# Rotated order of matmul groups over two array halves, value blocks ahead of projections, rings cleared later, in a fused attention and gated-MLP kernel

## Chip, cores and metric

One core of one Trainium2 chip runs the kernel. The metric is device time in microseconds (us) of one launch; a profiled execution gives a trace with every engine's instructions.

## The reference

For 2048 tokens of width 512 (x) the kernel mixes two branches with a gate per token, `g = sigmoid(sum(x * gate_w))`:

```python
qkv = x @ wqkv                       # 32 heads of 16
p = softmax(q k^T / 4) where 0 <= i - j < 256
a = (p @ v) @ wo
b = (sigmoid(x @ w_gate) * (x @ w_up)) @ w_down   # inner width 1376
out = g * a + (1 - g) * b
```

## The kernel before

Float32 precision comes from splitting: each operand is a rounded high part and a low remainder (`split`: ScalarE casts the high part, VectorE subtracts), and a product is three matmuls (`mm3`). A contraction of 512 is four slices d of 128 rows, so a 512-column result takes 12 matmuls.

Instructions stand in the order in which the code issues them on TensorE (PE), ScalarE (ACT), VectorE (DVE) and SyncE (SP), whose queue holds all DMAs; GpSimd (POOL) masks and fills. Tags of PSUM pools name banks: `s` 2, `st` 2, `misc` 3, `pv` 1.

*Opening.* 20 filler matmuls on zeros (`idle_mm`) run until data comes. SP loads query/key weights `wqk`, chunk 0 of x (512 tokens, four slices), the value weights `wv`, then chunks 1 to 3 of x, all but `wqk` into the space of the later value tile V. GpSimd clears three rings (`ring`, stacked query and key rows), then writes V's constant columns (`fill_v`). PE projects step 0 and step 4 (`proj_mm`, tiles pj), with fillers between, computes value blocks 0 to 3 (`v_block`, tiles vps) and goes on with projection 1. A projection step is 512 tokens of one group of four heads' queries and keys; pairs of steps are copied into a ring by `stack_build` through SP (from tiles sh and sl, high and low).

*Main loop.* Round u (0 to 139) has four sub-rounds hh. Each issues one score matmul group for the row maximum (`s_part`, tile s, VectorE reduces it) for u below 128, and from u = 9 (LAG) one transposed score (`st_part`, tile st, ScalarE's exponential into pt). GpSimd masks pt (`mask_p`); every second round `pv_part` multiplies by V into the bank pv.

*Filler stream.* Between these, `turns()` feeds groups of 12 matmuls: gate and up products (gu), further projections (pj) and the remaining width (tail, tp). Each contraction slice is cut in two halves of 64 rows; half 0 uses the upper half of the array's rows and half 1 the lower, and both add into one bank of tag misc. At step t half 0 does its step t, half 1 the step t - SHIFT; GAP = 3 steps go out per `next(slots)`. There are n_rest = 111 groups:

```python
for half, v in enumerate((t, t - SHIFT)):
    if 0 <= v < n_rest * k3:
        groups[v // k3][0](v % k3, half)
```

A group's result is taken off its bank (`post`) once half 1 is through: by ScalarE for gu and pj, put at the front of the list `acts`, of which one entry is issued per sub-round. `gu_next` then splits the next block's weights into the single weight tile w0. At the end the last three tail groups run undivided (`hold_group`), and the second matrix products (pd, pa) follow for 44 steps.

## Time and profile before

| | us |
|---|---|
| median of 3 runs (742.84 to 743.03) | 742.88 |
| profiled execution, own time | 743.2 |
| its span, first to last instruction | 741.5 |
| PE busy | 735.4 |
| VectorE busy | 505.3 |
| ScalarE busy | 432.2 |
| GpSimd busy | 173.9 |

Matmuls are pipelined and their ends are modelled: the time of one is read from the distance of starts, not from its length. Of a wait for several semaphores the profile names the last.

### The profile page before, as it was taken

The page shows a single profiled execution, that of the slowest core. Times are in us where ns is not written, and L with a number is a line of the kernel's source. Part 1 is how long each engine was busy: PE and PEld are TensorE (multiplying, and loading weights), DVE is VectorE, ACT ScalarE, POOL GpSimd, SP SyncE. Part 2 cuts the span into 40 slices and gives each one's busy share as a digit, 9 for nine tenths or more (in the row PEclk, how much of TensorE's full clock was granted, in tenths as well). Part 3 has the DMA queues.
Part 4 walks back from the last instruction along what each step waited for, and adds up shares of the span by engine and source line. Part 5 has one row for each costly group of instructions (what it writes and reads, how often), then busy time and mean ns, then how long its engine had stood idle before and what let it go on. Part 6 is the DMA issues. An engine that isn't in the chain of part 4 may idle for free.

```text
span 741.5 us, 17721 instructions
## 1 busy us (share of the span) xinstructions
PE 735.4 (99%) x6310; PEld 586.3 (79%) x6310; DVE 505.3 (68%) x1518; ACT 432.2 (58%) x921; POOL 173.9 (23%) x256
## 2 busy tenths in 40 slices
PE   9999999999999999999999999999999999999997
PEld 7889777787777877778777787778887878887886
DVE  5358767766776776776677677677745774848473
ACT  6422676666676666666666666666665662535341
POOL 7000333233233223323323322332341000000000
PEclk9999999999999999999999999999999999999999
DMA  8341434436444353443534425554277867879561
GB/s 299 102 120 30 108 96 119 128 85 166 122 107 127 106 147 111 115 130 96 155 111 120 122 72 155 154 140 138 72 267 221 238 174 193 203 180 228 146 133 58
DMA packets 94321, 103.66 MB, mean 140 GB/s; under 512 B 44926, under 2 KB 57214, under 8 KB 94232
## 3 DMA queue, kind: packets, MB, share of 16 engines
q1 hardware_dynamic: 94232, 102.53, 50.0%
q8 instruction: 49, 0.80, 0.4%
q14 instruction: 40, 0.33, 0.1%
HBM read 45.32 MB, written 31.99 MB: 104 GB/s over the span
## 4 chain that ended last, share of the span: by engine, by line
PE 96%; DMA 2%; DVE 1%; issue 0%; ACT 0%; SPq 0%; DVEq 0%
PE gu L247 28%; PE pv L394 12%; PE pj L247 11%; PE s L315 8%; PE tp L519 5%; PE st L361 5%; PE pd L80 5%; PE pd L78 5%; PE pd L79 5%; PE vh L556 3%; PE pa L78 2%; PE pa L79 2%; PE pa L80 2%; DMA V<-in_xT_dram 2%; PE vps L78 1%; PE vps L79 1%
## 5 line engine op out<-in xcount | busy, mean ns | idle before, releaser
L321 DVE CUSTOM_DVE_ANT_0 junk<-s,mask 128x384 f32<-128x384 f32 (+2 forms) x512 | 271.7, 531 | 125.5 <-PE s L315 68.5
L366 ACT ACTIVATE pt<-st 128x384 f32<-128x384 f32 (+2 forms) x512 | 240.2, 473 | 168.0 <-PE st L361 68.6
L247 PE MATMUL gu<-xh,w 64*128 64x512 f32 x1152 | 295.3, 393 | 0.0
L247 PE MATMUL gu<-xl,w 64*128 64x512 f32 x576 | 190.7, 392 | 0.0
L371 POOL TENSOR_SCALAR_AFFINE_SELECT pt<-pt 128x512 f32<-128x512 f32 x128 | 88.1, 688 | 372.4 <-ACT pt L366 372.4
L247 PEld LDWEIGHTS gu<-xh,w 64*128 64x128 f32 x1152 | 160.9, 185 | 14.1
L361 PE MATMUL st<-ring 64*128 64x384 f32 (+2 forms) x536 | 168.5, 332 | 0.2 <-ACT ring L121 0.2
L315 PE MATMUL s<-ring 64*128 64x384 f32 (+2 forms) x536 | 167.0, 329 | 0.4 <-DVE mx L321 0.4
L315 PEld LDWEIGHTS s<-ring 64*128 64x128 f32 x536 | 95.6, 184 | 37.7 <-DVE nm L331 12.5
L361 PEld LDWEIGHTS st<-ring 64*128 64x128 f32 x536 | 96.6, 184 | 9.9 <-issue 2.7
L247 PEld LDWEIGHTS gu<-xl,w 64*128 64x128 f32 x576 | 90.7, 185 | 3.7
L394 PE MATMUL pv<-pt,V 128*32 128x384 f32 (+2 forms) x1408 | 91.0, 389 | 0.0
L247 PE MATMUL pj<-xh,wqh 64*128 64x512 f32 (+1 forms) x228 | 89.1, 397 | 0.0
L247 PE MATMUL pj<-xl,wqh 64*128 64x512 f32 (+1 forms) x228 | 88.3, 393 | 0.2 <-DVE xl L75 0.2
L376 POOL TENSOR_SCALAR_AFFINE_SELECT pt<-pt 128x512 f32<-128x512 f32 x112 | 76.2, 680 | 0.0
L247 PE MATMUL pj<-xh,wql 64*128 64x512 f32 (+1 forms) x228 | 69.9, 392 | 0.0
L394 PEld LDWEIGHTS pv<-pt,V 128*32 128x32 f32 x1408 | 37.2, 109 | 35.5 <-issue 29.2
L78 PE MATMUL pd<-ring,hb 128*128 128x512 f32 x160 | 63.0, 394 | 0.0
L80 PE MATMUL pd<-ring,hb 128*128 128x512 f32 x160 | 63.0, 393 | 0.0
L79 PE MATMUL pd<-ring,hb 128*128 128x512 f32 x160 | 62.3, 390 | 0.0
L74 ACT CAST hb<-V 128x512 fp32r<-128x512 f32 x40 | 24.9, 622 | 52.5 <-DVE V L703 50.0
L247 PEld LDWEIGHTS pj<-xl,wqh 64*128 64x128 f32 (+1 forms) x228 | 41.7, 185 | 3.4 <-DVE xl L75 1.4
(122 smaller groups left out, 1145.9 us busy)
## 6 DMA issues: line engine op xcount, KB each, us to landing
gu_scratch<-sp SPq DMA_DIRECT2D x72, 256.0 KB
V<-gu_scratch SPq DMA_DIRECT2D x36, 512.0 KB
ring<-sh SPq DMA_DIRECT2D x128, 128.0 KB
ring<-sl SPq DMA_DIRECT2D x64, 128.0 KB
guraw<-in_wgu_dram SPq DMA_DIRECT2D x18, 256.0 KB
V<-in_xT_dram SPq DMA_DIRECT2D x16, 256.0 KB
oT_scratch<-ob SPq DMA_DIRECT2D x128, 32.0 KB
xl<-oT_scratch SPq DMA_DIRECT2D x16, 256.0 KB
```

Of the source, the lines that this page charges most:

```text
L78: mm(ps, lh, rh, start=first, stop=False)
L79: mm(ps, lh, rl, start=False, stop=False)
L80: mm(ps, ll, rh, start=False, stop=last)
L247: mm(pt, (wl if w == 2 else wh)[r, d], (xl if w == 1 else xh)[r, d, c * CH:(c + 1) * CH], start=k == 0 and half != 1, stop=k == 3 * ND - 1 ...
L315: mm(pt[:, (k - k0) * P:(e - k0) * P], lhsT, blk(g, k, hh, 1, e - k), start=k == k0, stop=e == i + 1, skip_group_check=True,)
L321: nc.vector.tensor_tensor_reduce(junk[:, 0:n], pt[:, 0:n], mask[:, 3 * P - n:], scale=1.0, scalar=NEG, op0=ALU.add, op1=ALU.max, accum_out ...
L361: mm(pt[:, (q - j) * P:(e - j) * P], lhsT, blk(g, q, hh, 0, e - q), start=q == j, stop=e == last, skip_group_check=True,)
L366: nc.scalar.activation(pts[u][:, hh, 0:n], pt[:, 0:n], AF.Exp, scale=SCALE)
L371: nc.gpsimd.affine_select(p[:, :, 0:P], p[:, :, 0:P], pattern=[[0, HG], [1, P]], compare_op=ALU.is_ge, fill=0.0, base=0, channel_multiplie ...
L376: nc.gpsimd.affine_select(p[:, :, 2 * P:], p[:, :, 2 * P:], pattern=[[0, HG], [-1, P]], compare_op=ALU.is_gt, fill=0.0, base=0, channel_mu ...
L394: mm(pv[32 * hh:32 * hh + 32, (q % 4) * P:(q % 4 + e - q) * P], V[:, j, h * VW:h * VW + 32], p[:, hh, (q - j) * P:(e - j) * P], start=Fals ...
L519: mm(tp[b][:, 0:TW], (xl if w == 1 else xh)[r, d, b * P:(b + 1) * P], tw[d][int(w == 2)][r, 0:TW], start=k == 0 and half != 1, stop=k == 3 ...
```

## The change

Three things. *Opening:* wv and chunk 0 of x are loaded slice by slice in turn, the first x slice in two halves; value blocks 0 to 3 go first, in four banks at once, slice by slice; projections 0 and 4 follow without fillers, and 16 fillers instead of 20 stand ahead. *Rings:* GpSimd clears them behind the first `fill_v`, and the constant rows (`fill_rows(t, 1, 1)`) are written with each ring's first `stack_build`. *Rotation:* SHIFT is 6 instead of 18, groups are taken three at a time, and a table TURN gives each half its own order in a triple, (0, 2, 1) and (1, 0, 2), so that the halves never work on one group at the same time; a group is done when both halves are through, whichever was first. With that, projections are asked for in pairs (`proj_at`), and some of the last odd rounds take 3 steps less.

```diff
-SHIFT = 18
+SHIFT = 6
+TURN = ((0, 2, 1), (1, 0, 2))
...
-        idle_mm(20)
-
-        raw_q = load_wqk(0)
-        load_x(0, range(0, 2))
-        split_wqk(0, raw_q)
-        raw_q = load_wqk(1)
-        load_x(0, range(2, ND))
-        split_x(0, range(0, 2))
-        split_wqk(1, raw_q)
-        split_x(0, range(2, ND))
+        idle_mm(16)
+
         for d in range(ND):
             nc.sync.dma_start(wvraw[:, d], wv_v[:, d])
             split(wvh[:, d], wvl[:, d], wvraw[:, d])
+            for h in range(2) if d == 0 else (None,):
+                ts = slice(0, CH) if h is None else slice(h * CH // 2, (h + 1) * CH // 2)
+                nc.sync.dma_start(xraw[:, 0, d, ts], xT_v[:, d, ts])
+                split(xh[:, d, ts], xl[:, d, ts], xraw[:, 0, d, ts])
+        raw_q = [load_wqk(g) for g in range(2)]
         load_x(1)
-        split_x(1)
         load_x(2)
-        load_x(3)
+        for g in range(2):
+            split_wqk(g, raw_q[g])
+        split_x(1, range(0, 2))
+        load_x(3, range(0, 2))
...
-        for r in range(RING):
-            nc.gpsimd.memset(ring[r].bitcast(F32), 0.0)
-            nc.sync.dma_start(*fill_rows(r, 1, 1))
...
         fill_v(0, NB // 2)
+
+        for r in range(RING):
+            nc.gpsimd.memset(ring[r].bitcast(F32), 0.0)
...
             dmas = [fill_rows(t % RING, 0, 0)]
+            if t < RING:
+                dmas.append(fill_rows(t, 1, 1))
...
-        for s, k0, k1 in ((0, 0, 4), (NC, 0, 4), (0, 4, 6), (NC, 4, 6), (0, 6, 12), (NC, 6, 12)):
-            for k in range(k0, k1):
+        vq = [ps.tile([P, D], F32, tag=t, name=f"vps{b}", bufs=n)
+              for b, (t, n) in enumerate((("s", 2), ("s", 2), ("st", 2), ("misc", 3)))]
+        for d in range(ND):
+            for w in range(3) if d < ND - 1 else (None,):
+                for b in range(4):
+                    bs = slice(b * P, (b + 1) * P)
+                    for v in range(3) if w is None else (w,):
+                        mm(vq[b], (xl if v == 2 else xh)[:, d, bs], (wvl if v == 1 else wvh)[:, d],
+                           start=d == 0 and v == 0, stop=d == ND - 1 and v == 2)
...
+        v_out(0)
+        split_x(1, range(2, 3))
+        v_out(1)
+        split_x(1, range(3, ND))
+        load_x(3, range(2, ND))
+        v_out(2)
+        v_out(3)
+        for s in (0, NC):
+            for k in range(3 * ND):
                 proj_mm(s, k)
-                if s == 0 and k < 4:
-                    idle_mm(1 + k % 2)
...
-                if t % k3 == 0 and len(groups) < n_rest:
-                    groups.append((work or rest).pop(0))
+                if t % (3 * k3) == 0 and len(groups) < n_rest:
+                    groups.extend((work or rest).pop(0) for _ in range(3))
                 for half, v in enumerate((t, t - SHIFT)):
                     if 0 <= v < n_rest * k3:
-                        groups[v // k3][0](v % k3, half)
...
+                        n, k = divmod(v, k3)
+                        n += TURN[half][n % 3] - n % 3
+                        groups[n][0](k, half, n in halves_done)
+                        if k == k3 - 1:
+                            halves_done[n] = halves_done.get(n, 0) + 1
+                            if halves_done[n] == 2:
...
+        proj_at = {5: [5], LAG: [6, 7], U_LAST: [NSTEP - 2], U_LAST + 1: [NSTEP - 1]}
+        for s in range(8, NSTEP - 2):
+            proj_at.setdefault(4 * s - (20 if s % 2 else 17), []).append(s)
...
-                    if u >= NU:
+                    if u >= NU and not (hh == HG - 1 and u % 2 == 1 and u > NU + 1):
                         next(slots, None)
```

The opening on PE, behind the first fillers; pj are projections, vps value blocks, w the high part of wv. Before:

```order
L247 MATMUL pj_183<-xh,wqh_111 128x512
L185 MATMUL warm_ps<-warm 128x256
L247 MATMUL pj_183<-xl,wqh_111 128x512
L185 MATMUL warm_ps<-warm 128x256 x2
L247 MATMUL pj_183<-xh,wqh_111 128x512
L185 MATMUL warm_ps<-warm 128x256
L247 MATMUL pj_183<-xl,wqh_111 128x512
L185 MATMUL warm_ps<-warm 128x256 x2
L247 MATMUL pj_194<-xh,wqh_123 128x512
```

and now:

```order
L438 MATMUL vps_173<-w_72,xh 128x512
L438 MATMUL vps_174<-w_72,xh 128x512
L438 MATMUL vps_175<-w_72,xh 128x512
L438 MATMUL vps_176<-w_72,xh 128x512
L438 MATMUL vps_173<-wvl,xh 128x512
L438 MATMUL vps_174<-wvl,xh 128x512
L438 MATMUL vps_175<-wvl,xh 128x512
L438 MATMUL vps_176<-wvl,xh 128x512
L438 MATMUL vps_173<-w_72,xl 128x512
```

Value blocks stand where projections and fillers were, four blocks to a slice.

The end of the filler stream on PE, ahead of and around the last transposed scores (st127); tp are tail groups. Before, half 1 ends alone:

```order
L361 MATMUL st126_1_9553<-ring_63 128x256
L519 MATMUL tp11_9432<-tail_hb0_7805,xh_70 128x450
L519 MATMUL tp11_9432<-tail_hb0_7805,xl_71 128x450
L519 MATMUL tp11_9432<-tail_hb0_7805,xh_70 128x450
L519 MATMUL tp11_9432<-tail_hb1_7806,xh_70 128x450
L519 MATMUL tp11_9432<-tail_hb1_7806,xl_71 128x450
L519 MATMUL tp11_9432<-tail_hb1_7806,xh_70 128x450
L361 MATMUL st126_2_9566<-ring_63 128x256
```

and now at the same place both halves run:

```order
L362 MATMUL st126_1_9546<-ring_63 128x256
L537 MATMUL tp11_9414<-tail_hb0_7814,xh_70 128x450
L537 MATMUL tp12_9442<-tail_wqh0_7810,xh_70 128x450
L537 MATMUL tp11_9414<-tail_hb0_7814,xl_71 128x450
L537 MATMUL tp12_9442<-tail_wqh0_7810,xl_71 128x450
L537 MATMUL tp11_9414<-tail_hb0_7814,xh_70 128x450
L537 MATMUL tp12_9442<-tail_wql0_7811,xh_70 128x450
L537 MATMUL tp11_9414<-tail_hb1_7815,xh_70 128x450
```

The 18 lone steps have become 6, of which three stand ahead of st127's first pair and three between its pairs. The matmuls of a step, one per half, follow each other, tp11 and tp12 in turn.

GpSimd's fillers, before:

```order
L217 MEMSET fr 1x1024
L220 MEMSET ring 128x4x1024 x3
L224 MEMSET V 128x8x16
L225 MEMSET V 128x8x32
L224 MEMSET V 128x8x16
```

and now:

```order
L217 MEMSET fr 1x1024
L220 MEMSET V 128x8x16
L221 MEMSET V 128x8x32
L226 MEMSET ring 128x4x1024 x3
L220 MEMSET V 128x8x16
```

The three ring fillers have moved behind the first pair of V's.

More of the change, by code (lines that the diff above doesn't have):

```diff
@@ L242, in gated_mix_kernel, with group_mm @@
         stg = {}
-        def group_mm(pt, wh, wl, c, k, half):
+        def group_mm(pt, wh, wl, c, k, half, second):
             d, w = divmod(k, 2) if k < 2 * ND else (k - 2 * ND, 2)
@@ L247, in group_mm, with proj_mm @@
             mm(pt, (wl if w == 2 else wh)[r, d], (xl if w == 1 else xh)[r, d, c * CH:(c + 1) * CH],
-               start=k == 0 and half != 1, stop=k == 3 * ND - 1 and half != 0,
+               start=k == 0 and not second, stop=k == 3 * ND - 1 and (half is None or second),
                skip_group_check=half is not None)
-        def proj_mm(s, k, half=None):
+        def proj_mm(s, k, half=None, second=False):
             g, c = divmod(s, NC)
@@ L254, in proj_mm @@
                 pj[s] = ps.tile([P, CH], F32, tag="misc", name=f"pj{s}", bufs=3)
-            group_mm(pj[s], *wq[g], c, k, half)
+            group_mm(pj[s], *wq[g], c, k, half, second)
         def proj_raw(s):
@@ L428, in v_block, with v_out @@
                 v_part(b, d)
-        for s, k0, k1 in ((0, 0, 4), (NC, 0, 4), (0, 4, 6), (NC, 4, 6), (0, 6, 12), (NC, 6, 12)):
-            for k in range(k0, k1):
+        vq = [ps.tile([P, D], F32, tag=t, name=f"vps{b}", bufs=n)
[7 more added lines that the diff above has]
+                           start=d == 0 and v == 0, stop=d == ND - 1 and v == 2)
+        def v_out(b):
+            nc.scalar.copy(Vh[:, b, :, 0:DH], vq[b].rearrange("p (h w) -> p h w", w=DH))
+        v_out(0)
[7 more added lines that the diff above has]
+            for k in range(3 * ND):
                 proj_mm(s, k)
-                if s == 0 and k < 4:
-                    idle_mm(1 + k % 2)
         proj_hi(0)
@@ L437, in gated_mix_kernel @@
         proj_raw(NC)
-        v_block(0)
-        v_block(1)
-        v_block(2)
-        v_block(3)
         proj(1)
@@ L473, in gated_mix_kernel, with gu_mm @@
         gp = {}
-        def gu_mm(f, c, w, k, half=None):
+        def gu_mm(f, c, w, k, half=None, second=False):
             if (f, c, w) not in gp:
                 gp[f, c, w] = ps.tile([P, CH], F32, tag="misc", name=f"gu{f}_{c}_{w}", bufs=3)
-            group_mm(gp[f, c, w], gv[:, 0, w], gv[:, 1, w], c, k, half)
+            group_mm(gp[f, c, w], gv[:, 0, w], gv[:, 1, w], c, k, half, second)
         def gu_post(f, c, w):
@@ L485, in gu_post @@
                 load_gu(f + 1, w)
+        gu_left = {}
         def gu_next(f, c, w):
-            if f + 1 < NFM and c == NC - 1:
+            gu_left[f, w] = gu_left.get((f, w), NC) - 1
+            if f + 1 < NFM and gu_left[f, w] == 0:
                 split_gu(f + 1, w)
@@ L512, in tail_split, with tail_mm @@
             behind.append(lambda: nc.vector.tensor_tensor(lo, raw, hi.bitcast(F32), op=ALU.subtract))
-        def tail_mm(b, k, half=None):
+        def tail_mm(b, k, half=None, second=False):
             if b not in tp:
@@ L519, in tail_mm @@
             mm(tp[b][:, 0:TW], (xl if w == 1 else xh)[r, d, b * P:(b + 1) * P], tw[d][int(w == 2)][r, 0:TW],
-               start=k == 0 and half != 1, stop=k == 3 * ND - 1 and half != 0,
+               start=k == 0 and not second, stop=k == 3 * ND - 1 and (half is None or second),
                skip_group_check=half is not None)
@@ L585, in gated_mix_kernel @@
             (
-                lambda k, h=None, a=(f, c, w): gu_mm(*a, k, h),
+                lambda k, h=None, x=False, a=(f, c, w): gu_mm(*a, k, h, x),
                 lambda a=(f, c, w): gu_next(*a),
@@ L591, in gated_mix_kernel @@
         ] + [
-            (lambda k, h=None, b=b: tail_mm(b, k, h), None, lambda b=b: tail_post(b)) for b in range(NB)
+            (lambda k, h=None, x=False, b=b: tail_mm(b, k, h, x), None, lambda b=b: tail_post(b)) for b in range(NB)
         ]
@@ L597, in proj_group @@
         def proj_group(s):
-            return lambda k, h=None: proj_mm(s, k, h), lambda: None, lambda: proj_out(s)
+            return lambda k, h=None, x=False: proj_mm(s, k, h, x), lambda: None, lambda: proj_out(s)
         def run_first(n):
@@ L614, in turns @@
             groups = []
+            halves_done = {}
             for t in range(n_rest * k3 + SHIFT):
@@ L617, in turns @@
                     yield
-                if t % k3 == 0 and len(groups) < n_rest:
-                    groups.append((work or rest).pop(0))
+                if t % (3 * k3) == 0 and len(groups) < n_rest:
+                    groups.extend((work or rest).pop(0) for _ in range(3))
                 for half, v in enumerate((t, t - SHIFT)):
                     if 0 <= v < n_rest * k3:
-                        groups[v // k3][0](v % k3, half)
-                if t >= SHIFT and (t - SHIFT) % k3 == k3 - 1:
-                    _, after, post = groups[(t - SHIFT) // k3]
-                    if after is None:
-                        post()
-                    else:
-                        acts.insert(0, lambda after=after, post=post: (post(), after()))
+                        n, k = divmod(v, k3)
[4 more added lines that the diff above has]
+                            if halves_done[n] == 2:
+                                _, after, post = groups[n]
+                                if after is None:
+                                    post()
+                                else:
+                                    acts.insert(0, lambda after=after, post=post: (post(), after()))
         def slot(h, d, c):
@@ L767, in gated_mix_kernel @@
                 nc.sync.dma_start(both, wo.rearrange("(c p) n -> p c n", p=P))
-            s4 = {5: 5, 9: 6, U_LAST: NSTEP - 2, U_LAST + 1: NSTEP - 1}.get(u)
-            if u % 4 == 3 and u > LAG and (u + 2) // 4 + 4 < NSTEP - 2:
-                s4 = (u + 2) // 4 + 4
-            if s4 is not None:
+            for s4 in proj_at.get(u, ()):
                 if u < LAG:
```

## Prediction

> **What bounds the kernel now.** First the page: its span and busy line, then the chain of work that ended last.

> ```profile
> span 741.5 us, 17721 instructions
> PE 735.4 (99%) x6310; PEld 586.3 (79%) x6310; DVE 505.3 (68%) x1518; ACT 432.2 (58%) x921; POOL 173.9 (23%) x256
> PE 96%; DMA 2%; DVE 1%; issue 0%; ACT 0%; SPq 0%; DVEq 0%
> ```

> TensorE is busy 99% of the span and carries 96% of the chain. A change pays here only if it takes instructions off TensorE's queue, or time in which that queue runs them alone, at half rate, or waits. A busy TensorE can be a slow one, so I next asked for the busy time by stage (time, PE, PEld, DVE, ACT, POOL, granted clock, DMA share, GB/s).

> ```profile
> 0.00:13.26 13.26, 11.76 (x50) 9.53 (x50) 6.87 (x11) 7.89 (x12) 12.51 (x12) 1.00 0.79 276
> 13.26:24.64 11.38, 11.26 (x50) 8.94 (x49) 3.56 (x6) 4.79 (x9) 1.59 (x3) 1.00 0.56 199
> 72.13:78.62 6.49, 6.09 (x36) 4.47 (x34) 5.95 (x19) 4.68 (x10) 1.93 (x2) 1.00 0.59 143
> 78.62:559.42 480.80, 480.59 (x5022) 379.03 (x5019) 339.92 (x1177) 317.40 (x720) 154.10 (x235) 1.00 0.44 126
> 559.42:564.96 5.54, 5.54 (x43) 3.96 (x40) 2.06 (x4) 2.71 (x9) 2.43 (x3) 1.00 0.69 210
> ```

> In the first 24.6 us TensorE does 72 useful matmuls; the main loop (78.6 to 559.4) has no gap; 72.1 to 78.6 and 559.4 to 565.0 are the two ends of the filler stream, where one array half has no partner. I went through those three places in the timeline.

> The opening (start, length, engine, line, operation, count):

> ```profile
> 1.25 4.64 PE L185 MATMUL warm_ps<-warm 128*128 128x256 f32 x20 [1.25 <-DVE warm L180]
> 3.62 0.62 ACT L153 CAST wqh<-wqraw 128x512 fp32r<-128x512 f32 x1 [1.54 <-DMA wqraw<-in_wqk_dram]
> 5.03 0.62 ACT L74 CAST xh<-V 128x512 fp32r<-128x512 f32 x1 [0.79 <-DMA V<-in_xT_dram]
> 5.70 0.80 PE L247 MATMUL pj<-xh,wqh 128*128 128x512 f32 x1
> 6.76 0.40 PE L185 MATMUL warm_ps<-warm 128*128 128x256 f32 x2
> 6.79 0.69 DVE L75 TENSOR_TENSOR xl<-V,xh 128x512 fp32r<-128x512 f32 x1 [0.42 <-ACT xh L74]
> 7.00 0.40 PE L247 MATMUL pj<-xh,wqh 128*128 128x512 f32 x1
> 7.24 0.62 ACT L153 CAST wqh<-wqraw 128x512 fp32r<-128x512 f32 x1 [0.47 <-DMA wqraw<-in_wqk_dram]
> 9.48 0.62 ACT L74 CAST xh<-V 128x512 fp32r<-128x512 f32 x1 [0.40 <-DMA V<-in_xT_dram]
> 10.15 2.66 ACT L74 CAST w<-V 128x512 fp32r<-128x512 f32 x4
> 16.51 0.19 PEld L78 LDWEIGHTS vps<-w,xh 128*128 128x128 f32 x1 [0.55 <-ACT pr L259]
> 24.64 0.19 PEld L247 LDWEIGHTS pj<-xh,wqh 128*128 128x128 f32 x1
> 25.02 2.72 PE pj L247 x12
> ```

> The first six 256 KB loads arrive about 1.2 us apart (casts waiting for them at 3.62, 5.03, ..., 7.24, ..., 9.48). From 10.15 on the casts follow each other without a wait. Twelve undisturbed matmuls take 2.72 us, 0.227 each. The 72 useful ones need 16.3 us; they begin at 5.70 and the next stage at 24.64, 18.9 later. So 2.6 us are lost to late splits, fillers between projections, a slow start and the 0.55 wait for a bank.

> **The change, part by part.** *Opening.* Now the four value blocks lead, 48 matmuls, ordered by the slice d of the contraction: 12 matmuls (2.72 us) per slice, while a slice needs two new loads, one of wv and one of x, 2.4 us at 1.2 apiece. Start: the 16 fillers at 4.64/20 = 0.232 end at 4.96. The first load's cast is over at 4.24; the first half of x's slice 0 comes between the first and second 256 KB, about 4.3, and its cast by 4.7 to 5.0. So the first useful matmul stands at about 5.0.

> It will still be slow. A 256-column filler takes 0.232 up to 5.7, but at 6.76 two of them take 0.24 together: the rate doubles near 6.3, though the granted clock says 1.00 throughout. From 5.0 to 6.3 matmuls cost 0.46 instead of 0.227, which loses 0.66 us. Slice 0 is done at 5.0 + 0.66 + 2.72 = 8.4. Slice 1 needs the fourth load, cast by 7.24 + 0.62 = 7.9; its low part 0.69 later is first used eight matmuls on. Slice 2 needs the sixth load, cast by 10.1, and PE comes at 11.1; slice 3 the eighth, which was there by 10.8, since from 10.15 nothing waited for loads seven to ten, and is cast by 11.4; PE comes at 13.8. No wait, with 0.5, 1.0 and 2.4 us in hand. Value blocks end at 16.6, the two projections (24 x 0.227) at 22.0: 2.6 before 24.64. Bounds: full rate at once, -3.3; half rate through all of slice 0, 12 x 0.46 = 5.5 instead of 3.4, which leaves -0.5.

> [...]

> What is moved off TensorE's path, at nothing:

> ```profile
> 3.73 10.45 POOL L220 MEMSET ring<- 128x4096 f32 x3
> 28.39 5.01 SPq L289 DMA_DIRECT2D ring<-sh  x8
> 33.50 2.47 SPq L289 DMA_DIRECT2D ring<-sl  x4
> 41.35 0.33 PE L315 MATMUL s<-ring 64*128 64x128 f32 x2
> ```

> GpSimd clears the rings after the value fillers, which wait for wv's last split (about 12.5): from 13 to 24 at 3.5 each, ring 0 at 16.8. SyncE writes ring 0 only after the second projection, now about 25.8, so it waits for that, not for the clear. Each ring's one extra fill is queued while SP waits there anyway. The first scores stood 5.4 us behind the last ring issue; both move forward by the same 2.6. If that cover went, each fill would cost one issue, about 0.6. x's last two loads now queue behind the splits of chunk 1, over near 16.5, and their casts come only after the second projection.

> *Rotation.* The filler stream has 12 x 111 + SHIFT steps, so 1350 become 1338. In the steady stream a step of both halves costs no more than one half alone:

> ```profile
> 72.53 0.39 PE L247 MATMUL pj<-xl,wqh 64*128 64x512 f32 x1
> 72.77 0.39 PE L247 MATMUL pj<-xh,wqh 64*128 64x512 f32 x1
> 306.05 0.34 PE L361 MATMUL st<-ring 64*128 64x384 f32 x1
> 306.23 0.39 PE L247 MATMUL gu<-xh,w 64*128 64x512 f32 x1
> 306.25 0.39 PE L247 MATMUL pj<-xl,wqh 64*128 64x512 f32 x1
> 306.46 0.39 PE L247 MATMUL gu<-xh,w 64*128 64x512 f32 x1
> 306.93 0.33 PE L315 MATMUL s<-ring 64*128 64x384 f32 x1
> 559.42 0.36 PE L519 MATMUL tp<-tail_hb,xh 64*128 64x450 f32 x1
> 559.62 0.36 PE L519 MATMUL tp<-tail_hb,xl 64*128 64x450 f32 x1
> ```

> A pair goes every 0.23 (306.23 to 306.46), a lone one every 0.24 at the start (72.53 to 72.77) and 0.20 at the end. Twelve steps fewer are thus 2.4 to 2.8. I take the end's price: the opening end lies where VectorE is busy 5.95 of 6.49 and sets the pace of a round, so there steps only move up and the saving falls due in the last rounds. 12 x 0.20 = 2.4, less 0.1 to 0.2: the last two pairs of transposed scores now have three lone matmuls between them (0.6) instead of six, and the second pair's bank waits for an exponential. So -2.3; bounds -2.8 and 0.

> At nothing: bank lifetimes (each bank of a triple is done after 30 steps and taken again at 36, as before); the weight splits, of which the tightest by the order (the sixth block's gate weights) stands five rounds of 0.88 (306.05 to 306.93) before its first reader, for 0.62 + 0.69 of work; and projections, which finish earlier or a little later but ahead of their ring writes. If the split's cover went, it would cost those 1.3 us once.

> The sum: -2.6 - 2.3 = -4.9. The profiled execution took 743.2, 741.5 of it span; the median of the runs is 742.88, 0.3 less. 743.2 - 4.9 = 738.3, so 738.0 by the median. About 0.2%, 1.5 us, is what a measurement tells from no change.

> **Rivals.** *Bank releases in bursts (slower).* Before, a bank came free every 12 steps; now three come free 6 steps apart, then a gap of 24. ScalarE empties them between exponentials.

> ```profile
> L366 ACT ACTIVATE pt<-st 128x384 f32<-128x384 f32 (+2 forms) x512 | 240.2, 473 | 168.0 <-PE st L361 68.6 <-PE s L315 56.4 <-POOL pt L376 37.1
> L482 ACT COPY sp<-gu 128x512 f32<-128x512 f32 x72 | 41.8, 581 | 0.0
> L247 PE MATMUL gu<-xh,w 64*128 64x512 f32 x1152 | 295.3, 393 | 0.0
> ```

> If one copy per triple stood an exponential too late, TensorE would wait 37 x 0.473 = 17.5: 743.2 - 4.9 + 17.5 - 0.3 = 755.5. It decides from 0.13 us a triple (4.9/37), and makes the kernel slower by over 0.2% from 0.17. Against it: the matmuls above show 0.0 idle, ScalarE is 58% busy, and each copy still stands one round behind its bank's last step with two or three rounds to the next use, as before. 7 in 100.

> *The opening stays slow.* The array keeps its half rate through slice 0, or the loads come as much later in the new order: 0.5 instead of 2.6, so 740.1. For it: fewer fillers, and only 0.5 us in hand at slice 1; against it: the rate doubled at 6.3 while the fillers had gaps. 10 in 100. [...]

> *The last rounds become GpSimd's.*

> ```profile
> 559.80 1.08 POOL L376 TENSOR_SCALAR_AFFINE_SELECT pt<-pt 128x512 f32<-128x512 f32 x1
> 561.66 0.96 POOL L371 TENSOR_SCALAR_AFFINE_SELECT pt<-pt 128x512 f32<-128x512 f32 x1 [0.78 <-ACT pt L366]
> 562.08 1.50 PE L394 MATMUL pv<-pt,V 128*32 128x384 f32 x16
> ```

> Masking runs close ahead of the value matmuls there, and odd rounds lose 3 steps, 0.6 us, of cover. If masks set the pace, the rotation gives 0: 740.3. Against it: the mask at 561.66 is for the pair after these value matmuls; theirs ended at 559.80 + 1.08 = 560.88, 1.2 us before, so 0.6 would be left. 9 in 100.

> *It doesn't shorten anything:* both gains go into such waits, say because the scores wait for ring 0 after all, about 742.9. 6 in 100. Better than -6.1: 2 in 100.

> **How the numbers follow.** The forecast, both terms within their bounds, has 66 in 100. Low is 742.9 - 3.3 - 2.8 = 736.8. High is 740.4, which takes in the two rivals in which one term is lost; left out are the bursts, no change, and the edge of the rest. Faster by over 0.2%: 66 + 10 + 9 + 2 = 0.87; within: 0.06; slower: 0.07.

> **What would show it.** Right: value matmuls from about 5.0 without a gap, the second projection near 22.0, first scores near 38.7; at both ends of the filler stream six lone steps; no TensorE idle time at gu, pj or tp; every stage from 80 on earlier by 2.6, and from 565 on by 4.9. Wrong: idle PE before the second or third slice; ScalarE's copies named as releaser of gu or pj; value matmuls of the last rounds waiting for GpSimd.

## The result, and the profile after

| us | before | after |
|---|---|---|
| median | 742.93 | 739.52 (738.69 to 741.25, 6 runs) |
| ratio, 95% interval | | 0.9954 [0.9937, 0.997] |
| profiled execution, own time | 743.2 | 740.04 |
| its span | 741.5 | 738.3 |
| median of a later session | 742.83 | 742.82 (740.66 to 743.97, 11 runs), ratio 0.9993 [0.9982, 1.0004] |

The forecast was 738.0, in 736.8 to 740.4. In the first measurement the change is faster by 0.46% and inside that range; in the later session the same kernel gains nothing and lies outside it, while the kernel before measured 742.8 to 743.3 in every session. So there are two things to explain: where part of the forecast gain went, and why the rest comes and goes.

The profile's page of the changed kernel, called after from here on: span, busy times, chain by engine and by line.

```profile
span 738.3 us, 17724 instructions
PE 731.9 (99%) x6300; PEld 578.7 (78%) x6300; DVE 507.8 (69%) x1519; ACT 431.2 (58%) x922; POOL 170.5 (23%) x256
PE 94%; DMA 2%; DVE 1%; ACT 1%; SPq 1%; issue 1%; DVEq 0%
PE gu L246 28%; PE pv L395 12%; PE pj L246 11%; PE s L316 7%; PE st L362 5%; PE pd L81 4%; PE pd L79 4%; PE pd L80 4%; PE tp L537 4%; PE vh L574 3%; PE pa L79 2%; PE pa L81 2%; PE pa L80 2%; PE vps L438 2%; DMA V<-gu_scratch 1%; DVE junk L322 1%
```

TensorE is as full as before, but a transfer, V<-gu_scratch, now stands in the chain. It brings the gate and up values of a step back from memory (`h_load`). 44 steps of second products (tiles pd) follow the main loop, 12 matmuls each, numbered from 0 here. ScalarE takes the sigmoid of what was loaded (L725) and casts the high part of the product, VectorE subtracts for the low part (both tile hb), and TensorE multiplies hb.

The opening in TensorE's timeline of after (start, length, engine, line, operation, count):

```profile
4.83 2.18 PE L438 MATMUL vps<-w,xh 128*128 128x512 f32 x4
6.85 1.08 PE L438 MATMUL vps<-wvl,xh 128*128 128x512 f32 x4
8.70 1.08 PE L438 MATMUL vps<-w,xh 128*128 128x512 f32 x4
17.02 0.40 PE L246 MATMUL pj<-xh,wqh 128*128 128x512 f32 x1
22.47 0.39 PE L246 MATMUL pj<-xh,wqh 128*128 128x512 f32 x1
38.96 0.33 PE L316 MATMUL s<-ring 64*128 64x128 f32 x2
```

Value matmuls run from 4.83 without a gap, the first four slowly (2.02 for four, then 0.92): at half rate, and the third's weight load waits 0.69 for ScalarE's cast of the slice's second half. The two projections start at 17.02 and the next one at 22.47. The first scores stand at 38.96, 2.39 earlier than the 41.35 of before, and the main loop keeps that distance up to 512 us.

The end of the filler stream, again TensorE's timeline of after, down to the first second product:

```profile
557.47 0.36 PE L537 MATMUL tp<-tail_hb,xh 64*128 64x450 f32 x1
...
557.88 0.37 PE L537 MATMUL tp<-tail_hb,xh 64*128 64x450 f32 x1
558.18 1.50 PE L395 MATMUL pv<-pt,V 128*32 128x384 f32 x16
559.60 0.33 PE L362 MATMUL st<-ring 64*128 64x128 f32 x2
559.77 0.42 PE L537 MATMUL tp<-tail_hb,xh 64*128 64x450 f32 x1
...
560.24 0.37 PE L537 MATMUL tp<-tail_hb,xh 64*128 64x450 f32 x1
569.19 0.50 PE L79 MATMUL pd<-ring,hb 128*128 128x512 f32 x1
```

Six lone steps are left. The same first second product stood at 573.58 before:

```profile
573.58 0.50 PE L78 MATMUL pd<-ring,hb 128*128 128x512 f32 x1
```

So 4.39 us are gained up to there, 2.39 ahead of the first scores and 2.00 behind them. Then some is given back. SyncE's queue (SPq), ScalarE's sigmoid of step 5 and TensorE's first matmul of step 5, from the timeline of after:

```profile
562.14 5.33 SPq L290 DMA_DIRECT2D xh<-tail_scratch  x6
570.94 0.50 SPq L290 DMA_DIRECT2D sum_scratch<-ob  x1
573.21 0.33 SPq L735 DMA_DIRECT2D sm<-sum_scratch  x1
576.14 0.45 SPq L673 DMA_DIRECT2D V<-gu_scratch  x1
581.95 0.63 ACT L725 ACTIVATE V<-V 128x512 f32<-128x512 f32 x1 [4.38 <-DMA V<-gu_scratch]
584.07 0.50 PE L79 MATMUL pd<-ring,hb 128*128 128x512 f32 x1 [0.59 <-ACT hb L75]
```

what SyncE's issues of after waited for from 560 to 582 (us in total, times, longest), the longest of them:

```profile
SPq L735 <- DMA sum_scratch<-ob: 1.5, 1, 1.5
```

the window 572 to 574 of after (columns as in the prediction, the last two the DMA share and GB/s):

```profile
572.00:574.00 2.00, 2.00 (x11) 1.63 (x10) 2.00 (x6) 1.15 (x2) 0.00 (x0) 1.00 0.08 26
```

and the same places in the timeline of before:

```profile
566.21 3.73 SPq L289 DMA_DIRECT2D xh<-tail_scratch  x6
573.47 0.50 SPq L289 DMA_DIRECT2D sum_scratch<-ob  x1
575.38 0.34 SPq L712 DMA_DIRECT2D sm<-sum_scratch  x1
578.41 0.45 SPq L650 DMA_DIRECT2D V<-gu_scratch  x1
583.80 0.63 ACT L702 ACTIVATE V<-V 128x512 f32<-128x512 f32 x1 [1.83 <-DMA V<-gu_scratch]
```

TensorE reaches this stage 4.4 earlier, the load of step 5 is issued only 2.27 earlier (576.14 for 578.41). The six reads of tail_scratch take SyncE 5.33 instead of 3.73. Then comes the last load of the softmax sums (sm, `sums_load(3)`): it reads what the sum store just ahead of it writes, so SyncE stands for 1.8 us (570.94 + 0.50 to 573.21), 1.5 of them for that store to land. As every transfer of the kernel is issued there, the DMA engines run empty (share 0.08 in that window). The load of step 5 is queued behind. Before, ScalarE waited 1.83 for it and TensorE not at all; now ScalarE waits 4.38 and TensorE is held up: 0.76 us are lost ahead of the first matmul of step 5, 0.45 within that step and 0.24 in step 6, together the 1.4.

### The profile page after: what moved, and what is told of

Its sections match the earlier page's. It is cut to its first block, busy times and chain, and to the rows that moved or that the text cites. A ratio compares the mean times of both kernels' runs of the same rounds, so it can differ in the third digit from the quotient of the medians.

```text
span 738.3 us, 17724 instructions
## 1 busy us (share of the span) xinstructions
PE 731.9 (99%) x6300; PEld 578.7 (78%) x6300; DVE 507.8 (69%) x1519; ACT 431.2 (58%) x922; POOL 170.5 (23%) x256
## 4 chain that ended last, share of the span: by engine, by line
PE 94%; DMA 2%; DVE 1%; ACT 1%; SPq 1%; issue 1%; DVEq 0%
PE gu L246 28%; PE pv L395 12%; PE pj L246 11%; PE s L316 7%; PE st L362 5%; PE pd L81 4%; PE pd L79 4%; PE pd L80 4%; PE tp L537 4%; PE vh L574 3%; PE pa L79 2%; PE pa L81 2%; PE pa L80 2%; PE vps L438 2%; DMA V<-gu_scratch 1%; DVE junk L322 1%
## 5 line engine op out<-in xcount | busy, mean ns | idle before, releaser
L246 PE MATMUL gu<-xh,w 64*128 64x512 f32 x1152 | 270.8, 393 | 0.0
L246 PE MATMUL gu<-xl,w 64*128 64x512 f32 x576 | 182.8, 392 | 0.0
L372 POOL TENSOR_SCALAR_AFFINE_SELECT pt<-pt 128x512 f32<-128x512 f32 x128 | 86.4, 675 | 373.6 <-ACT pt L367 370.1
L362 PE MATMUL st<-ring 64*128 64x384 f32 (+2 forms) x536 | 168.0, 332 | 0.1
L246 PEld LDWEIGHTS gu<-xh,w 64*128 64x128 f32 x1152 | 150.7, 185 | 13.5
L246 PEld LDWEIGHTS gu<-xl,w 64*128 64x128 f32 x576 | 87.5, 185 | 4.2
L246 PE MATMUL pj<-xl,wqh 64*128 64x512 f32 (+1 forms) x228 | 80.0, 392 | 0.0
L246 PE MATMUL pj<-xh,wqh 64*128 64x512 f32 (+1 forms) x228 | 79.8, 392 | 0.0
L377 POOL TENSOR_SCALAR_AFFINE_SELECT pt<-pt 128x512 f32<-128x512 f32 x112 | 74.7, 667 | 0.0
L75 ACT CAST hb<-V 128x512 fp32r<-128x512 f32 x40 | 24.9, 622 | 51.5 <-DVE V L726 48.9
L246 PEld LDWEIGHTS pj<-xh,wql 64*128 64x128 f32 (+1 forms) x228 | 41.2, 185 | 3.1
```

Of the source, the lines that this page charges most:

```text
L246: mm(pt, (wl if w == 2 else wh)[r, d], (xl if w == 1 else xh)[r, d, c * CH:(c + 1) * CH], start=k == 0 and not second, stop=k == 3 * ND - ...
L362: mm(pt[:, (q - j) * P:(e - j) * P], lhsT, blk(g, q, hh, 0, e - q), start=q == j, stop=e == last, skip_group_check=True,)
L372: nc.gpsimd.affine_select(p[:, :, 0:P], p[:, :, 0:P], pattern=[[0, HG], [1, P]], compare_op=ALU.is_ge, fill=0.0, base=0, channel_multiplie ...
L377: nc.gpsimd.affine_select(p[:, :, 2 * P:], p[:, :, 2 * P:], pattern=[[0, HG], [-1, P]], compare_op=ALU.is_gt, fill=0.0, base=0, channel_mu ...
```

## Experiments

Start of three things in each profile, against the profile of before: the first VectorE reduction of scores, the first and the last matmul of the second products. The median is of the run's own session; where it was timed, before measured 743.29 (e1 to e4), 742.83 (e5 to e8) and 743.17 (e9, e10).

| run | first scores | second products | their end | median, us |
|---|---|---|---|---|
| after | -2.39 | -4.39 | -2.97 | 739.52 |
| e1 opening and rings alone | -2.37 | -2.52 | -2.59 | 741.16 |
| e2 rotation alone | +0.08 | -1.39 | +1.33 | 743.43 |
| e3 after, AHEAD 6 | -2.08 | -2.53 | -1.42 | 741.68 |
| e4 before, AHEAD 6 | -0.23 | +0.75 | +0.71 | 744.31 |
| e5 rotation, sums late | -0.24 | -2.58 | -0.83 | 741.98 |
| e6 after, sums late | -1.36 | -3.92 | -3.97 | 739.06 |
| e7 before, sums late | -0.02 | -0.30 | -0.30 | 742.89 |
| e8 after again | -2.16 | -4.47 | -0.16 | 742.82 |
| e9 after, sums and tail reads late | -1.89 | -4.36 | -0.04 | 742.36 |
| e10 rotation, the same | 0.00 | -1.96 | +1.30 | 744.84 |
| e11 e6 with rings early | -1.21 | -3.00 | -2.21 | 740.82, one run |
| e12 after, 6 fillers | -0.51 | -2.91 | +1.01 | 744.01, one run |

**e1 and e2: the parts alone.** e1 takes the hunks of the opening and the rings, e2 all others.

> The kernel before with the new opening and the later ring clears alone (SHIFT stays 18, no table of turns). Theory (the opening gives 2.4 in the trace of the changed kernel, first scores at 38.96 instead of 41.35, and nothing behind it takes it back): 743.2 - 2.4 = 740.8 profiled, the second products from 569 on earlier by 2.4 as well, no stall of ScalarE on a gate/up load above the 1.8 us of before. Rival (the end is paced by SyncE's loads whatever TensorE does): the opening's gain is partly lost at the same place, 742.2, with ScalarE's wait for the load of step 5 above 3 us.

> The kernel before with the rotation alone (SHIFT 6, table of turns, projections in pairs, the 3 steps less in odd last rounds); the opening and the rings stand as before. Theory (rotation saves 2.0 up to the start of the second products, and then SyncE's queue, which moves up less, gives back most of it): earlier by 2.0 near 569, later by about 1.4 again between 580 and 590, 743.2 - 0.6 = 742.6 profiled, ScalarE's wait for the load of step 5 near 4 us. Rival (the loss in the changed kernel comes from both parts together, or from chance): 743.2 - 2.0 = 741.2 with that wait below 2 us.

e1: ratio 0.997 [0.9958, 0.9982], and its 2.4 reach the end; ScalarE's wait for the load of step 5 did grow, to 2.5, but TensorE did not stop for it. e2: 1.0002 [0.9989, 1.0014], single runs from 740.52 to 746.31, so neither its theory nor its rival gave the size. Its profile wins 1.5 in the last rounds and loses 2.7 behind them, more than the 1.4 expected. From the waits of e2 between 563 and 603 (us in total, times, longest):

```profile
ACT V L711 <- DMA V<-gu_scratch: 6.3, 3, 5.8
PE pd L79 <- ACT hb L75: 2.0, 1, 2.0
```

Only the rotation loses at step 5, and it does so without the opening.

**e3 and e4: one load more ahead.**

```diff
-AHEAD = 5
+AHEAD = 6
```

> The changed kernel with the gate/up loads of the second products asked for six steps ahead instead of five (AHEAD = 6), so that the load of step 5 stands in SyncE's queue in front of the last sum store and its wait. Theory (that load is what gives back 1.4): the second products start at 569 as now and no TensorE wait for hb follows, 740.0 - 1.4 = 738.6 profiled. Rival (the transfers themselves are the bound there, or the wait only moves to the load of step 6): 739.6 to 740.0, with the same idle time at another step.

> The kernel before with AHEAD = 6 alone. Theory (in the kernel before, TensorE did not wait at hb, so an earlier load hides nothing): 743.2 within 0.3. Rival (one more load ahead helps any kernel of this kind): faster by 1 us or more, 742.2 or less.

Theory and rival failed in both: e3 gains 0.9975 [0.9964, 0.9986] on before, but its 741.68 is above either, and e4 is slower, 1.0011 [1.0003, 1.002]. The first loads now stand ahead of the last row maxima in SyncE's queue. TensorE's only wait in e4 from 537 to 560, absent before (e3 has one of 1.3 of the same kind):

```profile
PE st L361 <- DMA ring<-max_scratch: 1.2, 1, 1.2
```

In e4 ScalarE's waits for the gate/up loads fell to 0.3 us in total; in e3 they come to 2.8, and a weight load of the second products waits 1.3 for VectorE's low part. Asking for the loads earlier only moved the loss to other places of the same queue, so the next edit moves the wait itself.

**e5 to e8: the sums' load behind the loads of steps 5 and 6, and the changed kernel once more.**

```diff
-            if SUMS <= u and (u - SUMS) % 4 == 0:
+            if SUMS <= u < N - 1 and (u - SUMS) % 4 == 0:
...
+            if n == 1:
+                sums_load(NC - 1)
             if n == 2:
                 gate()
+            if n == 5:
                 last_sums = sums_invert(NC - 1)
-            if n == 3:
+            if n == 6:
                 nc.sync.dma_start(*last_sums)
```

> The kernel with the rotation alone, and the last load of the softmax sums (sums_load(3)) asked for behind the gate/up load of step 6 instead of ahead of the load of step 5, its reciprocal and store three steps later. Theory (SyncE waits there for the last sum store to land, about 2.2 us, its DMA queue runs empty meanwhile, and the load of step 5 behind it holds TensorE up): the rotation alone measured 743.4 and its profile lost 2.7 between 582 and 592; without the wait that goes, 743.4 - 2 = 741.2 to 741.6, runs close together, no TensorE wait for hb at step 5. Rival (the transfers take the time whatever the order): 743 to 743.4 and the same scatter of several us.

> The changed kernel with sums_load(3) behind the load of step 6, likewise. Theory: all 4.4 that the profile of the changed kernel shows at 569 reach the end, 740.0 - 1.4 = 738.6 profiled and 738.2 to 738.7 in the median. Rival (the wait only moves to another load, as it did with AHEAD = 6): 739.5 to 740.

> The kernel before with sums_load(3) behind the load of step 6 alone. Theory (TensorE did not wait at hb in the profile of before, so nothing is to be gained): 743.3 within 0.4. Rival (the late load costs that kernel too): 742.2 or less.

> The changed kernel once more, beside the others on the same chip. Theory (the part that is lost at the late load differs from execution to execution, with the landing times): a median between 739 and 741 and runs spread over 2 us or more, against under 1.5 for e6. Rival (a fixed loss): all within 0.7 of 739.5.

On one chip: e8 742.82, e6 739.06 (0.9953 [0.9941, 0.9966]), e7 742.89 (1.0002 [0.9993, 1.0011]). The edit is worth nothing to the kernel before and 3.8 to the changed one; every run of e6 (738.29 to 740.25) is below every run of e8 (740.66 to 743.97). For e6 and e8 the expectations had the direction and not the size: e8 spreads over more than 2 us, as its theory said, but its median lies above the 739 to 741 expected; e6 spreads over 2.0, not under 1.5, and its median is 0.4 above the theory's range. The timeline of e8:

```profile
574.96 0.33 SPq L735 DMA_DIRECT2D sm<-sum_scratch  x1
577.89 0.45 SPq L673 DMA_DIRECT2D V<-gu_scratch  x1
583.45 0.63 ACT L725 ACTIVATE V<-V 128x512 f32<-128x512 f32 x1 [5.95 <-DMA V<-gu_scratch]
585.56 0.50 PE L79 MATMUL pd<-ring,hb 128*128 128x512 f32 x1 [2.17 <-ACT hb L75]
586.94 0.63 PE L80 MATMUL pd<-ring,hb 128*128 128x512 f32 x1
587.37 0.63 PE L81 MATMUL pd<-ring,hb 128*128 128x512 f32 x1
590.33 0.39 PE L79 MATMUL pd<-ring,hb 128*128 128x512 f32 x1
```

of e6:

```profile
571.63 0.50 SPq L290 DMA_DIRECT2D sum_scratch<-ob  x1
575.25 0.45 SPq L673 DMA_DIRECT2D V<-gu_scratch  x1
577.50 0.47 SPq L735 DMA_DIRECT2D sm<-sum_scratch  x1
580.05 0.63 ACT L725 ACTIVATE V<-V 128x512 f32<-128x512 f32 x1 [2.01 <-DMA V<-gu_scratch]
```

and by windows, two of e8 (574 to 576; 587 to 590, its granted clock third from the end), then one of e6:

```profile
574.00:576.00 2.00, 2.00 (x11) 1.63 (x10) 1.26 (x3) 1.15 (x2) 0.00 (x0) 1.00 0.02 8
...
587.00:590.00 3.00, 3.00 (x9) 2.32 (x8) 2.96 (x7) 2.54 (x5) 0.00 (x0) 0.50 0.83 265
```

```profile
574.00:576.00 2.00, 2.00 (x11) 1.63 (x10) 1.30 (x4) 0.76 (x3) 0.00 (x0) 1.00 0.83 201
```

In e8 the DMA engines stand still from 574 to 576, the load is late and TensorE stops for 2.2. From 586.94 to 590.33 its matmuls then start 0.43 apart instead of 0.23, at a granted clock of 0.50: after the pause the array ran at half rate for 3.4 us, and 8 matmuls by 0.2 cost another 1.6. That is how a load some 1.5 us later than in after takes back 4.3 instead of 1.4.

The mean granted clock of each run says how often this happens. One such stretch takes 3.41 x 0.5 / 741 = 0.0023 off it: the profiled executions of e8, e9 and e12, whose traces show one stretch each, have 0.997, 0.998 and 0.997. Of e8's 11 runs seven have 0.995 to 0.998 and a median span of 741.6 us, four have 0.999 or 1.0 and 739.45. In the first measurement all six runs have 0.999 or 1.0, with a median span of 737.8, and the five of e6 have such clocks too. So about half of the 3.3 us between the two measurements of the same kernel goes with the half rate; the other half is there without it.

In e6 the window has 0.83 DMA share, and nothing is lost (-3.92 to -3.97). e5 keeps a part only: 741.98, 0.9984 [0.9975, 0.9993], less than the 2 us expected. There the tail reads hold SyncE until 570.95, and ScalarE still waits 4.5 for step 5. So the wait for the sum store is not the only cause.

**e9 and e10: the tail reads later as well.**

```diff
-            if u == TREAD:
-                tail_reads(0)
-            if u >= TREAD:
-                tail_read(0, 3)
+            if u == N - 1:
+                tail_reads(0)
...
-            if f < 4:
-                tail_read(c, 2)
+            if f < 5:
+                tail_read(c, 2 if c else 3)
```

> The changed kernel with sums_load(3) behind the load of step 6 and, besides, the 12 reads of the tail (64 KB each) taken out of the last four rounds and spread over the first five steps of the second products, so that the gate/up loads of steps 3 and 4 are not queued behind them. Theory (the stretch is bound by SyncE's queue, in which the tail reads held SP for 5 us): the loads of steps 3 to 5 land before their sigmoid asks for them, no TensorE wait at hb, 738.0 to 738.8 in the median and runs within 1.5 us. Rival (the bytes have to be moved in any case, and the reads now collide with the loads of steps 5 to 9): 739.5 or more, with the wait at a later step.

> The kernel with the rotation alone and both of these moves. Theory: the rotation's 2.3 at the start of the second products reach the end: 743.0 - 2.3 = 740.7 in the median, no TensorE wait at hb above 0.5. Rival (a loss of another kind goes with the rotation): 742 or more, as with sums_load(3) moved alone.

The rival held: 742.36 for e9 (0.9986 [0.9977, 0.9995] of before), and 744.84 for e10, slower than before by 1.0023 [1.0012, 1.0033]. SyncE's queue and TensorE at step 8 in the timeline of e9, and its window 570 to 572:

```profile
568.05 0.50 SPq L290 DMA_DIRECT2D sum_scratch<-ob  x1
573.06 0.94 SPq L290 DMA_DIRECT2D tail_scratch<-tt  x2
574.09 0.41 SPq L673 DMA_DIRECT2D V<-gu_scratch  x1
594.82 0.80 PE L81 MATMUL pd<-ring,hb 128*128 128x512 f32 x1 [1.41 <-DVE hb L76]
```

```profile
570.00:572.00 2.00, 2.00 (x9) 1.65 (x10) 1.31 (x3) 1.15 (x2) 0.00 (x0) 1.00 0.00 0
```

SyncE now stands 4.5 us (568.05 + 0.50 to 573.06) until the last tail groups' results can be stored, with empty DMA engines, and the reads are issued among later loads; the loss is at steps 6 and 8, with half rate behind the second. Where the reads stood before, the same window had a DMA share of 0.95 in after and of 0.77 in e8.

**e11 and e12: the opening.** e11 is e6 with the rings cleared ahead of the value fillers again; in e12 `idle_mm(16)` is `idle_mm(6)`.

> The kernel of e6 with GpSimd's ring clears and their constant rows put back ahead of the value fillers, as in the kernel before. Theory (the clears lie behind other work in either place): first scores within 0.2 of e6 where the loads land alike (some 39 to 40), the TensorE timeline of the opening the same. Rival (the ring writes or the copies of the value blocks wait for GpSimd): first scores later by 1 us or more, with GpSimd as the releaser.

> The changed kernel with 6 fillers instead of 16 ahead of the first value matmul (TensorE idle from 2.6 to about 4.8). Theory (the array runs at half rate until it has been busy some 5 us, as the doubling at 6.4 to 6.8 after a start at 1.25 shows): half rate lasts longer, the first doubling at 8.5 to 10, and the projections behind the value blocks start 1 to 2 us later than the 17.0 of the changed kernel. Rival (the rate doubles at a fixed time after the start, fillers or not): value matmuls as before, projections at 17.0 within 0.3.

TensorE's timeline of e11, then e12:

```profile
9.77 1.19 PE L437 MATMUL vps<-w,xh 128*128 128x512 f32 x4 [1.25 <-ACT xh L75]
18.20 0.40 PE L247 MATMUL pj<-xh,wqh 128*128 128x512 f32 x1
```

```profile
4.75 1.22 PE L438 MATMUL vps<-w,xh 128*128 128x512 f32 x2 [1.85 <-ACT xh L75]
7.28 1.91 PE L438 MATMUL vps<-wvl,xh 128*128 128x512 f32 x4
...
10.57 1.09 PE L438 MATMUL vps<-w,xh 128*128 128x512 f32 x4
18.90 0.40 PE L246 MATMUL pj<-xh,wqh 128*128 128x512 f32 x1
```

In e11 projections come 1.18 later than in after and first scores 1.18 later: all of it is the wait for x's second slice, and the clears add nothing behind it. Against e6, whose loads also came late, the first scores are 0.15 later, within the 0.2 expected. GpSimd releases nothing there, so the move of the clears gained nothing. In e12, one profile, the half rate lasts to about 10.4 instead of 6.8 (a little longer than expected, and beyond the 6.1 to 7.5 of nine profiles with 16 or 20 fillers), and projections come at 18.90, 1.9 late. That is in line with the theory of e12 and not with its rival; what sets the length is not shown.

## Why the prediction was right, and where it failed

- *Opening, forecast -2.6.* Measured -2.39 in the profile of after. The first matmul stood at 4.83 (5.0 said) and there was no gap. The mis-sized term is the slow start: the first four matmuls took 2.02, 1.1 more than at 0.227 each, where 0.66 was added. The half rate lasted to 6.8 and not 6.3, and the third weight load waited 0.69 for a cast. The sum hid 0.2 of that, as it counted from a weight load at 24.64 and the matmul behind it started at 24.86. Over the seven profiles with the new opening and 16 fillers the mean is -1.9: the slice with only 0.5 in hand made TensorE wait 0 in after, 0.26 in e8, 0.73 in e6, 1.25 in e11. The bounds (-3.3 to -0.5) held in each.
- *Rotation, forecast -2.3.* Measured -2.0 in after, and between -1.5 and -2.6 over the eight profiles with it and AHEAD 5 and 16 or 20 fillers; kernels without it drift by -0.2 in the same stretch. Six lone steps were at the end, as forecast. One wait was not: in eight profiles with the rotation (after, e5, e6, e8 to e12) score matmuls wait for VectorE's row maxima twice, 0.7 us in total, in before and e7 once, 0.4. The wait that is new, 0.33, stands at 514.19 in after, and the distance to before shrinks by 0.4 there. The forecast had no term for VectorE in that stretch; what brings the wait is not shown.
- *Everything from 565 on earlier by 4.9: this step failed.* The sum gave the transfers at the end no term. It took the second products to move with TensorE, and costed SyncE's queue in the opening only. The prediction's own row showed a DMA share of 0.69 from 559 to 565, where 2 us of cover were to go. Measured: -4.4 at the start of the second products, -3.0 at their end in after, -0.2 in e8. In its place the runs show SyncE's wait for the sum store, the late load of step 5 behind it, and in e8 the half rate behind the pause.
- *Why the number fitted.* In part by luck: 739.5 is within range because the profiled execution gave back only 1.4 and the mean clocks of that measurement's runs leave no room for a stretch at half rate. With 4.3 given back, the same kernel measured 742.8, above the high end.
- *Bursts.* The group below (busy, mean ns, idle) shows 0.0 idle time again, and the distance of -2.4 is constant from 70 to 512.
- *The others.* The slow opening appeared in part, as the second slice's wait; its reason "fewer fillers" rested on no run then, and later the half rate lasted to about 10.4 with the 6 of e12, for 6.8 with the 16 of after. GpSimd: no value matmul of the last rounds waits for a mask. "It doesn't shorten anything" had 6 in 100 and is what e8 shows in its median, by a wait in a place that the prediction had not costed.

The group of gu in after, as in the prediction:

```profile
L246 PE MATMUL gu<-xh,w 64*128 64x512 f32 x1152 | 270.8, 393 | 0.0
```

What stays open: why the load of step 5 lands 1 to 2 us later in some executions. In e8 the tail reads held SyncE 6.24 us and in after 5.33; what slows these transfers is not shown. The sessions of e1 to e4, e5 to e8 and e9 to e12 ran on three different chips, and the chip of the first measurement is not on record, so chip and session cannot be told apart. e6 is the fastest version measured, but five runs of one session, and e11, which shares its queue order, lost 0.8 there in its one profile.

## What to carry to other kernels

Time taken off the busiest engine is worth only as much as the queues that feed it can follow: of the 4.4 us here 3.0 reached the end in after and 0.2 in e8. Before summing up a gain, look at each in-order queue in the stage that inherits it, and in that queue for a wait on a store just issued. In e6 a load that reads back such a store did better behind loads that wait for nothing (739.06 for the 742.82 of e8); e7 shows that this is worth nothing where the loads had cover (742.89 for 742.83). And measure such an end in more than one session, since the wait and the half rate behind it come and go from run to run (mean clocks of 0.998 or less in seven of e8's 11 runs, in none of the six of the first measurement).

## What the hardware showed beside that

In e8, e9 and e12 a pause of TensorE cost more than itself. Start distances of second products around the pause: 2.57 in e8 and 2.41 in e12 were followed by 3.41 us at half rate, 1.6 us extra; so were the two of 0.92 and 1.79 close together in e9; 2.40 in e2 was not, nor 1.80 in e10 or 0.99 in after. So the length of the pause alone does not decide it. In the opening of nine profiles with 16 or 20 fillers (before, after, e2, e4 to e6, e8, e9, e11) the first matmul at the full rate started between 6.1 us (e4) and 7.5 us (e9).
